# Reciprocals from a second scan that runs backwards, first-group inputs in homes of their own, and F of four units ahead of k's work

## The chip, the core and the metric

The kernel runs on one core of one Trainium2 chip. Such a core has a matrix engine (PE, with its weight loads listed apart as PEld), a vector engine (DVE), an activation engine (ACT), a general engine (POOL) and a queue engine (SP) that mostly issues DMAs; ACT can issue DMAs too. Each engine works through its own instructions in program order and waits on semaphores for the others. The metric is device time in microseconds, the median of three runs.

## The reference, cut to what matters

A recurrent attention block feeds a wide feed-forward layer. All is float32; the two weight matrices arrive as float64 words and are turned into float32 on the chip.

```
state = zeros(B, H, D, D)                      # B = 4, H = 8, D = 40
for t in range(768):
    y[t]  = r[t] @ state
    Sa    = state @ a[t]
    state = state * w[t] - outer(Sa, b[t]) + outer(v[t], k[t])
x = y as (B*S, H*D) = (3072, 320)
h = x @ w_in                                   # 320 x 2048
out = (h * clip(h + 3, 0, 6) / 6) @ w_out      # 2048 x 320
```

## The kernel before, in words

**Blocks and units.** Time is cut into blocks of 64 steps. A unit is one block of two batches, all eight heads; four units make a group, and there are 24 units in six groups. Inside a block the recurrence is rewritten with matrices: running products of w (the decays) scale a, b, k and r, the products of scaled a and b give a strictly triangular matrix F for each head, and the state's contribution needs the inverse of one plus F.

**Preparing a unit (`prepare`, lines 469 to 630).** The stages have names. W transposes w on PE, copies it into a padded tile `wm` and takes running products with a scan (line 485), `prods`. Before the change the rows of 32 steps each begin with an element that is 0 in `wm` and 1 in `start`, so one scan of 528 elements restarts in 16 rows. gam makes two tiles: `gam`, whose first half of each block is a reciprocal of products (line 496) and whose second half is a copy on POOL (497), and `rgam`, whose first half is a copy on POOL (498) and whose second half is a reciprocal (511, issued in stage A). A multiplies the transposed a by `gam` (514), B the transposed b by `rgam` (522), K the transposed k by `rgam` (606). F multiplies the results of A and B on PE (536) and copies to the tile F on ACT (542). factor turns `rgam` back and multiplies k and b with it on POOL (591). E and EV are a masked product (465) and its product with v.

**Inverting (`invert`, line 646).** Once the F of four units is there, DVE transposes it in 32 by 32 blocks (`fb`, 651), POOL masks it into `x` (654), and 60 small DVE instructions (663 and 669, in turn) invert all 32 triangles of 32 by 32 together; two more transposes give `tb` and `tt` (672, 677). `third_block` (688) then makes the missing corner of each 64 by 64 inverse on PE, ACT and POOL. The small instructions depend on one another, so others are dealt between them.

**Converting the weights (`load_weights`, line 257).** Twenty pieces of `w_in` and `w_out` are fetched as 64-bit words into spare places and converted, each by four DVE instructions (301, 321, 325, 312) and two on ACT (302, 304). A call of `next(weights)` issues one step with one of the DVE instructions. The spare places include parts of `win`, `wout`, `tinv` and of the pool `inv`. The tile of `inv` with the tag `x` is used in turn for the second set of w and a, for the matrix of the inversion and for a raw piece.

**What sets the order at the start.** Nothing is planned at run time: the order in which Python emits instructions is the order on each engine. `by_twos` (1099) walks the first group's four units through their stages, two units ahead of the other two, and appends the inversion once F of all four is emitted. From then on `aside` emits a step of the inversion at a time, and with a weight of `MIXED` a share of a conversion step. The loop at 1142 runs the inversion to its end; the numbers in `STEPS` say after which of its steps a conversion step follows. `PLAN` then lists the steps of the first group's four units (`0U` is stage U of unit 0, X and Y the two `third_block`s) and after a colon how many conversion steps follow each. From line 10 of the plan on the second group is prepared by the same `by_twos`, with feed-forward work (`pieces`) between. Later groups follow in `a_block`, in whose `together` the order of the results is the list `RESULTS`.

**Inputs.** `fetch` (383) issues two DMAs for w, a, b or k of a unit and four for r or v, on SP unless told otherwise. In the first two groups there are two sets of input tiles, for even and odd units, so the loads of units 2 and 3 are issued when units 0 and 1 have been transposed (`following`, 407). v of the first group is fetched in stage K.

Of the kernel before, what the change touches and what calls it, by code (L numbers as in the profile page):

```python
# [16 lines left out]
P = 128  # L17
BL = 64
# [12 lines left out]
def kernel(  # L31
# [145 lines left out]
    wm = const.tile([P, SCAN], F32, name="wm")  # L177
    nc.vector.memset(wm[:], 0.0)
# [40 lines left out]
    ]  # L219
    win = wts.tile([P, 2, DFF], F32, name="win")  # L220
    win2 = wts.tile([P, DFF // 2], F32, name="win2")
    wout = wts.tile([P, NJ, DM], F32, name="wout")
    WC = 256
# [159 lines left out]
    def fetch(name, i, engine=None):  # L383
# [5 lines left out]
        if name == "V":  # L389
            t = values[i % AHEAD]  # L390
        else:
            t = (others if i < 2 * NU and i % 2 and name != "R" else inputs)[name]
# [14 lines left out]
    def following(i):  # L407

        if i < 2 * NU:

            return i + 2 if i % NU < NU - 2 or i % 2 == 0 else None
        return i + 1
# [56 lines left out]
    def prepare(i, F):  # L469
        n, o = i % NU, data[i]  # L470
        halves = i >= 2 * NU
        def w_stage():
# [3 lines left out]
            wv = wm[:].rearrange("p (r m i) -> p r m i", m=2, i=HB + 1)  # L476
            x = wt[:].rearrange("p r (q m i) -> p (r q) m i", q=2, m=2)
            nc.scalar.activation(out=wv[:, :, 0, 1:HB + 1], in_=x[:, :, 0, ::-1], func=AF.Copy)
            if i == 0:
                nc.vector.tensor_copy(wv[:, :, 1, 1:HB + 1], x[:, :, 1, :])  # L480
            else:
# [4 lines left out]
                out=prods[:].rearrange("p r m i -> p (r m i)"), data0=wm[:], data1=start[:],  # L486
# [3 lines left out]
        def gam_stage():  # L490

            gam = o["G"] = grp.tile([P, NPR, P], F32, name="gam", tag="gam", bufs=NU + 2)
            rgam = o["rg"] = tmp.tile([P, NPR, P], F32, name="rgam", bufs=2)
            gv = gam[:].rearrange("p r (q i) -> p (r q) i", q=2)
            rv = rgam[:].rearrange("p r (q i) -> p (r q) i", q=2)
            nc.vector.reciprocal(gv[:, :, 0:HB], o["prods"][:, :, 0, 1:HB + 1][:, :, ::-1])  # L496
# [10 lines left out]
        def a_stage():  # L507
            x = turn_in(o["AN"], halves)
            yield PE
            rv = o["rg"][:].rearrange("p r (q i) -> p (r q) i", q=2)  # L510
            nc.vector.reciprocal(rv[:, :, HB:BL], o["prods"][:, :, 1, 1:HB + 1])  # L511
# [88 lines left out]
        def k_stage():  # L600
            x = turn_pairs(o["KN"])
            yield PE
            if i < NU:
                fetch("V", i)
            kt = o["kt"] = turned("kt")
            nc.vector.tensor_tensor(out=kt[:], in0=x[:], in1=o["rg"][:], op=ALU.mult)
# [81 lines left out]
    def third_block(F, tb, tt, n, first=False):  # L688


        zs = tmp.tile([P, 2, H, L], F32, name="zs")
# [44 lines left out]


# [361 lines left out]
    def by_twos(first, steps, mixed, rate):  # L1099
# [3 lines left out]
        for t in range(TWOS):  # L1103
# [3 lines left out]
            if t < 2:  # L1107
                order = [0, 0, 1, 1][4 * t:]
# [12 lines left out]
    for name in "WABK":  # L1121
        for i in range(2):
            fetch(name, i, (nc.sync, nc.scalar) if name == "W" else None)
    for t, _ in enumerate(by_twos(0, 4, MIXED, 0)):
        if t == 5:
            next(weights)
        limit[0] = {7: 4, 10: 12}.get(t, limit[0])
        while t == 7 and refill[0]():
            pass
        if t == RFETCH:  # L1130
            fetch("R", 0)
    ring.clear()
# [7 lines left out]
    STEPS = (1, 4, 7, 9, 12, 16, 17, 22, 27, 28, 32, 33, 34, 41, 44, 46, 51, 61, 64)  # L1140
# [15 lines left out]
    firsts = [third_block(*third[-1], n, True) for n in (0, 2)]  # L1156

    def block(i, j):

        if i % NU < 2:  # L1160
            if j == 0:
                n = i % NU
                blocks[i] = third_block(*third[-1], 2 * n)
# [4 lines left out]
    PLAN = """X X 0U:3 0UT:1 1R  # L1168
              0sn:1 0H:2 Y:1
              1U 1UT:3 0y:2  # L1170
              2RT:2 Y
              1sn 1H:1 2VT:1 0move 0move2
              1y:2 2R
              2S:1 3RT
              1move 1move2 2U:3 2UT:2 2C:4
              3R:4 3VT:3
              2rS:3 2sn:3 2H:3 3S:3
              2y:3 3U:4 3UT:2 3C:5
              3rS:3 3sn:3 3H:3 2move
              3y:1 2move2  # L1180
# [32 lines left out]
    for _ in range(18):  # L1213
# [15 lines left out]
    RESULTS = ["RT", "y", "W", "gam", "VT", "EV", "R", "S", "C", "A", "B", "move", "move2",  # L1229
               "U", "UT", "rS", "F", "K", "sn", "H", "E", "factor"]  # L1230
# [132 lines left out]
```

## Time and profile before

| what | us |
|---|---|
| median of three runs (lowest, highest) | 821.16 (818.71, 823.44) |
| the profiled execution | 820.82 |
| its span, first to last instruction | 819.1 |
| busy: PE, PEld | 742.1, 630.1 |
| busy: DVE, ACT, POOL | 534.2, 321.1, 152.4 |

The span is 1.7 us shorter than the profiled execution's time, which includes what lies around the instructions. PE is busy for 91% of the span, but not evenly: the first sixth of the span has PE mostly waiting, and after it PE is nearly full. Times inside the span are counted from its start. A group's row gives the total busy time, then the mean duration of one instruction in nanoseconds, then the idle time ahead of it with what ended that wait.

### The profile page before, as it was taken

The page shows a single profiled execution, that of the slowest core. Times are in us where ns is not written, and L with a number is a line of the kernel's source. Part 1 is how long each engine was busy: PE and PEld are TensorE (multiplying, and loading weights), DVE is VectorE, ACT ScalarE, POOL GpSimd, SP SyncE. Part 2 cuts the span into 40 slices and gives each one's busy share as a digit, 9 for nine tenths or more (in the row PEclk, how much of TensorE's full clock was granted, in tenths as well). Part 3 has the DMA queues.
Part 4 walks back from the last instruction along what each step waited for, and adds up shares of the span by engine and source line. Part 5 has one row for each costly group of instructions (what it writes and reads, how often), then busy time and mean ns, then how long its engine had stood idle before and what let it go on. Part 6 is the DMA issues. An engine that isn't in the chain of part 4 may idle for free.

```text
span 819.1 us, 35789 instructions
## 1 busy us (share of the span) xinstructions
PE 742.1 (91%) x15832; PEld 630.1 (77%) x15832; DVE 534.2 (65%) x1090; ACT 321.1 (39%) x847; POOL 152.4 (19%) x297
## 2 busy tenths in 40 slices
PE   4633858989999989999999999999999999999998
PEld 4532757868877878788888888878888888888886
DVE  8899688778855679745699564798546685232210
ACT  2233664222455423645333644334562434332211
POOL 4232101320122130322121222113112102000000
PEclk9755687999999999999999999999999999999999
DMA  6763562341223330332231233132232101100000
GB/s 111 153 150 92 122 137 59 65 67 26 42 50 62 57 62 14 60 56 48 44 57 31 46 67 56 30 57 39 41 61 53 19 20 29 29 19 16 17 19 16
DMA packets 174218, 45.05 MB, mean 55 GB/s; under 512 B 157424, under 2 KB 172784, under 8 KB 174064
## 3 DMA queue, kind: packets, MB, share of 16 engines
q1 hardware_dynamic: 171840, 42.36, 27.0%
q8 instruction: 125, 2.05, 1.1%
q10 hardware_dynamic: 2224, 0.41, 0.3%
q14 instruction: 29, 0.24, 0.1%
HBM read 34.08 MB, written 3.93 MB: 46 GB/s over the span
## 4 chain that ended last, share of the span: by engine, by line
PE 71%; issue 9%; DVE 8%; DMA 5%; SPq 3%; POOL 2%; ACT 1%; DVEq 0%; POOLq 0%; ACTq 0%
PE h L977 24%; PE o L1018 22%; PE any L456 4%; PE any L892 3%; PE any L418 3%; PE any L868 2%; PE any L428 2%; SPq L404 2%; PE any L812 1%; DVE x L669 1%; DVE prod L663 1%; PE any L773 1%; PE any L849 1%; PE any L833 1%; SPq L401 1%
## 5 line engine op out<-in xcount | busy, mean ns | idle before, releaser
L977 PE MATMUL h<-xt,win 128*128 128x128 f32 (+1 forms) x2304 | 251.6, 283 | 9.2 <-DVE gt L993 9.2
L977 PEld LDWEIGHTS h<-xt,win 128*128 128x128 f32 (+1 forms) x2304 | 232.0, 192 | 26.3 <-DVE gt L993 7.7
L1018 PE MATMUL o<-wout,gt 128*128 128x320 f32 x768 | 230.8, 444 | 0.0
L1018 PEld LDWEIGHTS o<-wout,gt 128*128 128x128 f32 x768 | 138.7, 190 | 50.5 <-issue 0.4
L992 ACT ACTIVATE gt<-h,three 128x512 f32<-128x512 f32 x96 | 62.1, 685 | 100.5 <-PE h L977 100.2
L993 DVE SCALAR_TENSOR_TENSOR gt<-gt,h 128x512 f32<-128x512 f32 x96 | 61.5, 677 | 58.4 <-ACT gt L992 57.3
L877 DVE TENSOR_TENSOR state<-any,state 40x160 f32<-40x160 f32 (+1 forms) x88 | 27.9, 321 | 67.8 <-PE any L868 41.6
L663 DVE TENSOR_TENSOR prod<-x 128x30 f32<-128x30 f32 (+9 forms) x180 | 62.3, 346 | 13.7 <-POOL x L654 8.3
L907 POOL TENSOR_TENSOR yg<-ys,gam 128x512 f32<-128x512 f32 x22 | 39.2, 1780 | 170.9 <-DVE ys L905 87.2
L669 DVE TENSOR_TENSOR x<-x,prod 128x30 f32<-128x30 f32 (+9 forms) x180 | 64.5, 359 | 5.8 <-DVE prod L663 0.5
L591 POOL TENSOR_TENSOR KBt<-K,rgt 128x320 f32<-128x320 f32 x24 | 20.9, 871 | 238.4 <-ACT rgt L581 223.6
L465 DVE COPY_PREDICATED score<-mask,any 128x256 f32<-128x256 int32 x143 | 53.3, 436 | 3.6 <-PE any L456 3.2
L496 DVE RECIPROCAL gam<-prods 128x256 f32<-128x256 f32 x24 | 41.8, 1749 | 13.6 <-POOL yg L907 13.2
L511 DVE RECIPROCAL rgam<-prods 128x256 f32<-128x256 f32 x24 | 41.8, 1743 | 0.0
L626 ACT ACTIVATE EV<-any 64x160 f32<-64x160 f32 x92 | 24.8, 296 | 40.5 <-PE any L620 31.1
L905 DVE TENSOR_TENSOR ys<-any,ys 128x256 f32<-128x256 f32 x44 | 16.6, 419 | 34.3 <-PE any L620 18.3
L485 DVE TENSOR_TENSOR_SCAN prods<-wm,start 128x528 f32<-128x528 f32 x24 | 30.0, 1248 | 10.4 <-ACT wm L482 9.9
L752 ACT ACTIVATE RT<-any 128x256 f32<-128x256 f32 (+1 forms) x44 | 15.5, 401 | 51.9 <-PE any L428 49.6
L892 PE MATMUL any<-score,KBt 64*64 64x64 f32 x1536 | 30.9, 231 | 0.2 <-DVE bt L522 0.2
L732 ACT ACTIVATE tinv<-any 32x256 f32<-32x256 f32 x48 | 17.9, 374 | 29.7 <-PE any L722 27.9
L892 PEld LDWEIGHTS any<-score,KBt 64*64 64x64 f32 x1536 | 27.2, 144 | 2.9 <-issue 0.7
L778 DVE TENSOR_TENSOR RR<-any,EV 128x160 f32<-128x160 f32 x44 | 12.2, 318 | 25.6 <-PE any L456 25.5
(181 smaller groups left out, 1058.4 us busy)
## 6 DMA issues: line engine op xcount, KB each, us to landing
B<-in_b_dram SPq DMA_DIRECT2D x48, 80.0 KB
K<-in_k_dram SPq DMA_DIRECT2D x48, 80.0 KB
V<-in_v_dram SPq DMA_DIRECT2D x96, 40.0 KB
out_dram<-ob SPq DMA_DIRECT2D x47, 80.0 KB
R<-in_r_dram SPq DMA_DIRECT2D x92, 40.0 KB
A<-in_a_dram SPq DMA_DIRECT2D x40, 80.0 KB
W<-in_w_dram SPq DMA_DIRECT2D x39, 80.0 KB
xt<-yg SPq DMA_DIRECT2D x72, 40.0 KB
```

Of the source, the lines that this page charges most:

```text
L456: nc.tensor.matmul(out=o[i][half(q), n, :], lhsT=lhs[half(i, D), n ^ (2 * q * swap), half(q)], rhs=rhs[half(i, D), n, half(q)], start=True ...
L465: nc.vector.copy_predicated(out=x[:, 4 * i:4 * i + 4, :], mask=mask4, data=o[i])
L496: nc.vector.reciprocal(gv[:, :, 0:HB], o["prods"][:, :, 0, 1:HB + 1][:, :, ::-1])
L511: nc.vector.reciprocal(rv[:, :, HB:BL], o["prods"][:, :, 1, 1:HB + 1])
L663: nc.vector.tensor_tensor(out=pv, in0=_ap(x[:], (i + 1) * L + i, [[L, n], [0, i]]), in1=_ap(x[:], i * L, [[0, n], [1, i]]), op=ALU.mult,)
L669: nc.vector.tensor_tensor(out=rest, in0=rest, in1=pv, op=ALU.add)
L892: nc.tensor.matmul(out=y[q][half(s), pr, :], lhsT=o[name][half(q), h * D:h * D + SLOT], rhs=m[name][half(q), 4 * rs + 2 * s + j, :], start ...
L907: nc.gpsimd.tensor_tensor(out=yg[:], in0=m["ys"][:].rearrange("p r q t -> p r (q t)"), in1=o["G"][:], op=ALU.mult)
L977: nc.tensor.matmul(out=hp[c][:, i, :], lhsT=lhsT, rhs=rhs, start=(begun[c] == 0), stop=(begun[c] == 3 * NQ - 1))
L992: nc.scalar.activation(out=gt[:], in_=hp[c][:], func=AF.Relu, bias=three[:], scale=1.0)
L993: nc.vector.scalar_tensor_tensor(out=gt[:], in0=gt[:], scalar=6.0, in1=hp[c][:], op0=ALU.min, op1=ALU.mult)
L1018: nc.tensor.matmul(out=op[:], lhsT=gts[c][:, n, :], rhs=wout[:, c * HJ + r * NQ + n, :], start=((split or r == 0) and c == 0 and n == 0), ...
```

## The change

Four edits go together.

1. **Reciprocals.** A second tile `wm` is added, and each has one element more. The reciprocals of 16 row ends (strided, one instruction) are written into the row heads of `start`; a scan over `wm` from its last element to its first, in place, multiplies each back by the w's; a `memset` puts the ones back. Two multiplications by 1.0 copy the results into the halves of `gam` and `rgam` that were reciprocals of 256 elements, and in stage A a `memset` of 33 elements clears the row heads of `wm`. In `RESULTS`, gam moves to the end. For unit 0 both copies of w into `wm` are made on DVE.
2. **Homes for the first group.** w, a, b and k of units 2 and 3 go into parts of `win` and `wout` that are not yet converted, their `rgam` into `win2`; four POOL memsets fill the pads. All loads of the first group are issued at the start, those of units 0 and 1 on SP and ACT alternately, and those of v after the others or between them.
3. **Order of the first group.** Lists replace `by_twos`: W, gam, A, B and F of all four units first, then the inversion begins, with K, factor, E and EV beside it.
4. **Third blocks and dealing.** The scratch `zs` of the two third blocks becomes one tile with two parts, with the tag `x`; `STEPS` has 15 numbers in place of 19, and the counts in `PLAN` are new.

```diff
+    wms = [const.tile([P, SCAN + 1], F32, name=f"wm{i}") for i in range(2)]
+    for t in wms:
+        nc.vector.memset(t[:], 0.0)
...
+    placed = {}
...
+    for i, (x, y) in enumerate([(0, DFF // 2), (0, NJ // 2)]):
+        for n, z in enumerate((x, y)):
+            t = win[:, :, z:z + H * SLOT] if i == 0 else \
+                wout[:, z:z + 4, :].rearrange("p j m -> p (j m)")[:, 0:2 * H * SLOT].rearrange(
+                    "p (n x) -> p n x", n=2)
+            t = t.rearrange("p n (h e) -> p n h e", e=SLOT)
+            name = ("WA", "BK")[i][n]
+            nc.gpsimd.memset(t[:, :, :, D:], PADS.get(name, 0.0))
+            for u in range(2):
+                placed[name, 2 + u] = t[:, u]
+    for u in range(2):
+        t = win2[:, u * NPR * P:(u + 1) * NPR * P]
+        placed["rgam", 2 + u] = t.rearrange("p (r t) -> p r t", t=P)
...
     def following(i):
 
+        if i < 2:
+            return None
...
-            nc.scalar.activation(out=wv[:, :, 0, 1:HB + 1], in_=x[:, :, 0, ::-1], func=AF.Copy)
+            if i == 0:
+                nc.vector.tensor_copy(wv[:, :, 0, 1:HB + 1], x[:, :, 0, ::-1])
+            else:
+                nc.scalar.activation(out=wv[:, :, 0, 1:HB + 1], in_=x[:, :, 0, ::-1], func=AF.Copy)
...
         def gam_stage():
 
+            prods, wm = o["prods"], o["wm"]
+            first = start[:].rearrange("p (n i) -> p n i", i=HB + 1)[:, :, 0]
+            nc.vector.reciprocal(first, prods[:].rearrange("p r m i -> p (r m) i")[:, ::-1, HB])
+            back = _ap(wm[:], SCAN, [[-1, SCAN]])
+            nc.vector.tensor_tensor_scan(out=back, data0=back, data1=start[:], initial=0.0,
+                                         op0=ALU.mult, op1=ALU.add)
+            nc.vector.memset(first, 1.0)
...
-            nc.vector.reciprocal(gv[:, :, 0:HB], o["prods"][:, :, 0, 1:HB + 1][:, :, ::-1])
+            row = 2 * (HB + 1)
+            nc.vector.tensor_scalar(gv[:, :, 0:HB], _ap(o["wm"][:], HB + 1, [[row, NB], [-1, HB]]), 1.0, None, ALU.mult)
+            nc.vector.tensor_scalar(rv[:, :, HB:BL], _ap(o["wm"][:], HB + 3, [[row, NB], [1, HB]]), 1.0, None, ALU.mult)
...
-            rv = o["rg"][:].rearrange("p r (q i) -> p (r q) i", q=2)
-            nc.vector.reciprocal(rv[:, :, HB:BL], o["prods"][:, :, 1, 1:HB + 1])
+            nc.vector.memset(_ap(o["wm"][:], 0, [[HB + 1, 2 * NB + 1]]), 0.0)
...
-            if i < NU:
-                fetch("V", i)
...
+    def third_blocks(first=False):
+
+        zs = inv.tile([P, 2, 2, H, L], F32, name="zs", tag="x", bufs=1)
+        return [third_block(*third[-1], 2 * n, zs[:, n], first) for n in range(2)]
...
-    for name in "WABK":
-        for i in range(2):
-            fetch(name, i, (nc.sync, nc.scalar) if name == "W" else None)
-    for t, _ in enumerate(by_twos(0, 4, MIXED, 0)):
-        if t == 5:
-            next(weights)
-        limit[0] = {7: 4, 10: 12}.get(t, limit[0])
-        while t == 7 and refill[0]():
+    for group, first in ("WAB", 0), ("WAB", 2), ("K", 0), ("V", 0), ("K", 2), ("V", 2):
+        for name in group:
+            for i in range(first, first + 2):
+                fetch(name, i, (nc.sync, nc.scalar) if first == 0 and name != "V" else None)
+    FIRST = "0W 1W 0gam 1gam 0A 1A 2W 3W 0B 1B 0F 1F 2gam 3gam 2A 3A 2B 3B 2F 3F".split()
+    BESIDE = "0K 1K 0factor 1factor 0E 1E 2K 3K 2factor 3factor 0EV 1EV 2E 3E 2EV 3EV".split()
+    chains = [in_turn(prepared(i), [x[1:] for x in FIRST + BESIDE if x[0] == str(i)]) for i in range(NU)]
+    for x in FIRST:
+        run(chains[int(x[0])])
+    side.append(invert(group_F[-1], third, True))
+    next(weights)
+    for n, x in enumerate(BESIDE):
+        limit[0] = {0: 4, 8: 12}.get(n, limit[0])
+        while n == 0 and refill[0]():
             pass
-        if t == RFETCH:
+        if n == 1:
             fetch("R", 0)
+        run(chains[int(x[0])], 1, MIXED if n >= 12 else 0)
...
-    STEPS = (1, 4, 7, 9, 12, 16, 17, 22, 27, 28, 32, 33, 34, 41, 44, 46, 51, 61, 64)
+    STEPS = (1, 6, 8, 9, 10, 14, 17, 25, 31, 36, 42, 48, 58, 61, 64)
...
-    firsts = [third_block(*third[-1], n, True) for n in (0, 2)]
+    firsts = third_blocks(True)
...
-    PLAN = """X X 0U:3 0UT:1 1R
-              0sn:1 0H:2 Y:1
-              1U 1UT:3 0y:2
-              2RT:2 Y
-              1sn 1H:1 2VT:1 0move 0move2
-              1y:2 2R
-              2S:1 3RT
-              1move 1move2 2U:3 2UT:2 2C:4
-              3R:4 3VT:3
-              2rS:3 2sn:3 2H:3 3S:3
-              2y:3 3U:4 3UT:2 3C:5
-              3rS:3 3sn:3 3H:3 2move
-              3y:1 2move2
+    PLAN = """X X:2 0U:3 0UT 1R
+              0sn 0H:2 Y:2
+              1U:1 1UT:3 0y:4
+              2RT:2 Y
+              1sn 1H 2VT:2 0move 0move2
+              1y:3 2R
+              2S:3 3RT
+              1move 1move2 2U:1 2UT 2C:6
+              3R:3 3VT
+              2rS:3 2sn:3 2H:4 3S:2
+              2y:2 3U:3 3UT:7 3C:5
+              3rS:4 3sn 3H 2move
+              3y 2move2
...
-    RESULTS = ["RT", "y", "W", "gam", "VT", "EV", "R", "S", "C", "A", "B", "move", "move2",
-               "U", "UT", "rS", "F", "K", "sn", "H", "E", "factor"]
+    RESULTS = ["RT", "y", "W", "VT", "EV", "R", "S", "C", "A", "B", "move", "move2",
+               "U", "UT", "rS", "F", "K", "sn", "H", "E", "factor", "gam"]
```

## The prediction, made before the changed kernel was run

> **What bounds the kernel now.** I read the slices of the page first, then the windows of ten microseconds, then DVE's timeline, last the waits. The windows (length, busy time of PE, PEld, DVE, ACT, POOL, then the granted PE clock and the DMA share) split the run in two:
>
> ```profile
> 20.00:30.00 10.00, 5.70 (x229) 4.61 (x212) 10.00 (x12) 3.38 (x12) 4.80 (x11) 1.00 0.53 80
> 30.00:40.00 10.00, 7.45 (x189) 6.21 (x193) 6.03 (x11) 1.52 (x5) 1.44 (x3) 0.55 1.05 219
> ...
> 60.00:70.00 10.00, 3.29 (x70) 2.58 (x68) 9.62 (x29) 4.19 (x7) 0.00 (x0) 0.50 0.47 97
> ...
> 90.00:100.00 10.00, 8.01 (x267) 7.19 (x266) 5.90 (x17) 5.44 (x11) 1.01 (x3) 0.66 0.70 159
> 100.00:110.00 10.00, 7.02 (x153) 6.37 (x152) 9.76 (x23) 7.65 (x14) 0.27 (x1) 0.83 0.38 91
> ...
> 190.00:200.00 10.00, 10.00 (x74) 8.49 (x73) 9.38 (x24) 1.26 (x2) 0.00 (x0) 1.00 0.04 9
> ```
>
> Until 77 us DVE is the bound: full from 10 to 30 and 40 to 80, PE mostly waiting. From 80 to 130 no engine is full: DVE is busy 36.3 of 50 us. From 140 on PE works 659.0 of 679 us; outside the last window it idles only 16.2. Of DVE time saved after 140 little can be had; the front end counts nearly in full, because the PE work behind it stays the same.
>
> DVE's timeline shows what the front consists of:
>
> ```profile
> 6.38 1.26 DVE L485 TENSOR_TENSOR_SCAN prods<-wm,start 128x528 f32<-128x528 f32 x1
> 7.67 1.75 DVE L496 RECIPROCAL gam<-prods 128x256 f32<-128x256 f32 x1
> ...
> 21.63 3.36 DVE L496 RECIPROCAL gam<-prods 128x256 f32<-128x256 f32 x2
> 24.90 1.04 DVE L465 COPY_PREDICATED score<-mask,any 128x256 f32<-128x256 int32 x3
> ...
> 33.02 0.69 DVE L606 TENSOR_TENSOR kt<-any,rgam 128x512 f32<-128x512 f32 x1 [0.55 <-PE any L418]
> 35.68 2.12 DVE L651 STREAM_TRANSPOSE fb<-F 128x1024 f32<-128x1024 f32 x1 [1.96 <-ACT F L542]
> 39.22 0.20 DVE L663 TENSOR_TENSOR prod<-x 128x30 f32<-128x30 f32 x1 [1.42 <-POOL x L654]
> ...
> 74.79 1.95 DVE L677 STREAM_TRANSPOSE tt<-x 128x1024 f32<-128x1024 f32 x1
> ```
>
> The inversion starts at 35.68 (`fb`) and ends at 76.6 (`tt` with the next start). Ahead of it stand eight reciprocals of 1.67 us start to start, and four multiplications for K and four masks that F doesn't need.
>
> [...] line 301, 512 elements, takes 0.42 us, tensor_tensor of 512 0.68. [...] the trace has 528 elements in 1.25 us. [...] while POOL multiplies for factor (41.7 to 45.5), a 108-element sum of line 669 takes 0.68 us after 0.51 idle, against 0.27 at 70.51, and line 325 takes 1.34 against 0.69. [...] the windows show 0.50 to 0.55 from 30 to 90.
>
> **Part 1, reciprocals.** Per unit two of 1.67 us go: 3.34. In their place: a reciprocal of 16 elements (256 take 1.75, a copy of 256 0.42, so some 6 ns an element and a fixed part: 0.2), a scan of 528 (1.22 start to start), a memset of 16 (0.06, line 176 has 0.07), two multiplications of 256 ([...] I take 0.27) and a memset of 33 (0.07). Sum 2.1; bounds 1.9 to 2.4. I assume that reading backwards costs nothing; no backward scan is in this trace. If it were twice as dear, 1.2 more, the gain of this part would be zero; I exclude that it speeds up. The scan[...] can now collide with POOL's three copies (0.40, 0.40, 0.21): up to 0.7 a unit, nothing at best; I take 1.0 for four units. The extra memset of `wm` (0.5) lies in DVE's idle time before 5.92.
>
> **Part 2, loads.** The w of unit 0 lands as before (PE starts at 4.38). Its two copies on DVE in turn (0.42 each, from 5.5) put the first scan at 6.4, as now. ACT issues eight DMAs at about 0.69 us from 1.1 to 6.7; unit 1's copies queue behind them and are done by 7.5, when the scan of unit 0 ends: hidden, and if late, at most 1 us. SP issues 6 + 12 + 2 + 8 + 4 + 8 = 40: 24 at 0.69 and 16 for v at 0.77 make 28.9, so the last leaves at 29.7. Now the first raw weights are issued at 29.58, so they are no later. w of units 2 and 3 leaves about 5 to 7.8 and is needed about 14; b about 10.5 to 13, needed about 22. The four pad memsets (some 1.6 us by those of 192 elements at 0.20 start to start) sit on POOL behind 6.5, ahead of unit 0's copies; these end about 9.2 and are needed for A at about 13. If PE or SP has to wait for the pads it is for something due later still.
>
> **Part 3, F first.** From 6.4: four scans 4.8, four gam parts 8.1, four memsets with A 0.63 + 0.56 x 4 ≈ 2.5, four B 2.4, collisions 1.0, in total 18.8: the last B ends at 25.2. F on PE (0.9 to 1.0) and ACT (0.66) with handovers take 1.8, so `fb` starts at 27.0 instead of 35.68: gain 8.7. The 1.42 us wait for POOL's mask is filled by two of K's multiplications.
>
> From `fb` to the end of `tt` it is 40.9 now. Two more multiplications of K (1.3) and four masks (1.4) come into it: +2.7. Of conversion steps, 19 lie there now, 9.1 us (0.48 each). After: 16 asides at the first group leave 47 numbered steps of which eleven are in `STEPS`, and the share of `MIXED` gives one: 12, so 7 fewer, -3.4. POOL's factor work doubles to eight multiplications beside the inversion; the present four cost DVE some 2.0 by the stretched rows, so +2.0. E's masks wait for PE at half clock: +0.8. Net +2.1: `tt` ends at 70.0, gain 6.6.
>
> **Part 4, plan.** The seven steps move into it: 7 x 0.53 = 3.7 us of DVE. It idles 13.7 of 50 us there, but steps in front of a mask or sum delay PE; I take half, 1.9. By the counts, the 80 steps end in the plan's line 12, not 11. A raw piece with the tag `x` now waits for the second use of `zs`; on SP, R of unit 3 stands behind it, needed three lines on: nothing, unless Y is late. Gain at the second group: 4.7.
>
> **Later units.** Twenty units save 1.2 us of DVE each, 24 us. Behind PE this is worth little: of the 16.2 us of idle, waits for DVE are part:
>
> ```profile
> PE any L620 <- issue: 4.5, 3, 3.1
> PE h L977 <- DVE gt L993: 3.6, 3, 1.3
> PE any L456 <- issue: 2.9, 3, 1.3
> ```
>
> I take 2.0; nothing to 5 is possible. Sum: 4.7 + 2.0 = 6.7 us. 820.8 (profiled execution, span 819.1 and 1.7 around it) less 6.7 is 814.1; the median stands 0.3 above the profiled one: 814.5.
>
> **Rivals.** (a) *Larger gain, 27%.* Conversion in the plan is free in DVE's idle time and later stalls close: 6.6 + 4 = 10.6, perhaps 13; about 810. For it: 13.7 us idle. Against it: ACT, which the steps load with 1.45 us a piece, is what PE waits for there (3.9 us at line 456 for U).
> (b) *No difference, 17%.* Conversion, with its DMAs, is the bound between 77 and 132 whenever the inversion ends; it now waits for raw pieces at 118 (2.9) and 123.6 (1.2). Were its end to stay at 132, the gain would be the later 2 at most: about 819.5. Against it: pieces are released by earlier conversions, which move forward too.
> (c) *Slower, 11%.* In later groups gam comes last of a stage's results, and its chain of reciprocal, scan and copies is serial; if it ends after PE's transposes of a, A and all behind it slip. The front's 6.7 is lost, and 4.1 more, when PE waits over 10.8 us in 20 units, 0.54 each; at 0.7 each the time is about 828. Against it: DVE has 35% free and the chain is 1.2 shorter than today's.
> (d) *The likeliest, 45%*: 811 to 817.
>
> The chances of (a) and (d), less a little at the edge, make 0.71 for faster by over 0.5%, about what a measurement can tell here (below 817.1); within it 0.18, slower 0.11. Range 805 to 821: below it is the far end of (a), 0.07, above it (c) and part of (b), 0.13. The bounds of scan and collisions (2 to 4 us) lie inside.
>
> **What would show it.** Backward scans of 1.25 us, multiplications of 0.2 to 0.33; `fb` at 27, `tt` ending at 70, twelve conversion steps between; the second group's first scan near 130 instead of 135.1; PE idle after 140 a little below 16. Wrong if `fb` starts after 30 because SP or ACT is late, if DVE stretches beside POOL by more than 4 us, or if the plan takes over 62 us instead of 58.5.

## The result, and the profile after

The changed kernel takes 814.54 us (median of five runs, 811.77 to 815.05). The kernel before took 821.28 in the five runs beside it. The ratio is 0.9906, with a 95% interval from 0.9876 to 0.9935: faster by 6.7 us between the medians, where 6.7 had been predicted; the interval of the ratio means 5.3 to 10.2 us, so the match to a tenth says little. Its profiled execution took 812.7 us, with a span of 811.0 (820.82 and 819.1 before). One execution of a kernel below (after, old reciprocals) was disturbed and took 2260.75 us; it is left out of that kernel's times, and its landmarks come from a second profile.

Where the time went is seen best in landmarks, in us from the span's start. The lead is how much earlier than before.

| landmark | before | after | lead | lead predicted |
|---|---|---|---|---|
| inversion starts (`fb`) | 35.68 | 26.94 | 8.7 | 8.7 |
| inversion ends (start of `tt` and its duration) | 76.7 | 71.6 | 5.1 | 6.6 |
| second group's first scan | 135.1 | 127.5 | 7.6 | 4.7 |
| second group's inversion starts | 176.2 | 171.2 | 4.9 | |
| third to sixth group's inversion starts | 287.8, 401.0, 519.5, 639.4 | 282.1, 394.2, 511.0, 631.3 | 5.7, 6.8, 8.5, 8.1 | |
| end of the span | 819.1 | 811.0 | 8.1 | 6.7 |

The windows of ten microseconds of the kernel after (length, busy time of PE, PEld, DVE, ACT, POOL, then granted PE clock, DMA share and GB/s):

```profile
20.00:30.00 10.00, 6.96 (x193) 6.29 (x182) 8.00 (x18) 2.85 (x8) 0.71 (x1) 0.88 0.49 73
30.00:40.00 10.00, 6.94 (x255) 6.38 (x250) 9.33 (x24) 3.34 (x13) 7.83 (x16) 0.97 0.64 131
60.00:70.00 10.00, 0.11 (x9) 0.14 (x13) 9.45 (x27) 1.44 (x2) 0.13 (x1) 0.50 0.07 10
90.00:100.00 10.00, 7.17 (x206) 6.16 (x206) 8.82 (x22) 6.87 (x15) 0.58 (x3) 0.83 0.70 178
100.00:110.00 10.00, 10.00 (x242) 9.61 (x241) 9.14 (x22) 7.45 (x15) 0.93 (x3) 0.83 0.36 92
```

POOL's factor work of all four units now lies beside the inversion (7.83 of 10 us from 30 to 40). From 60 to 70 PE has nothing to do. From 90 to 100 DVE is busy 8.82 where it was 5.90: the conversion steps that left the inversion fill its idle time, and DVE is now busy 43.7 of the 50 us from 80 to 130, where it was 36.3, so 6.3 of the 13.7 us of idle time are left.

DVE's timeline of the kernel after (start, duration, line, operation; in brackets the idle time ahead and what ended it):

```profile
9.88 0.26 DVE L516 RECIPROCAL start<-prods 128x16 f32<-128x16 f32 x1
10.17 1.26 DVE L518 TENSOR_TENSOR_SCAN wm<-wm,start 128x528 f32<-128x528 f32 x1
11.49 0.28 DVE L526 TENSOR_SCALAR gam<-wm 128x256 f32<-128x256 f32 x1
...
26.94 2.14 DVE L679 STREAM_TRANSPOSE fb<-F 128x1024 f32<-128x1024 f32 x1 [1.85 <-ACT F L572]
...
41.26 0.43 DVE L316 TENSOR_SCALAR parts<-tinv 128x512 uint32<-128x512 uint32 x1 [1.08 <-DMA tinv<-in_moe_w_in_dram]
58.29 0.78 DVE L483 COPY_PREDICATED score<-mask,any 128x256 f32<-128x256 int32 x2 [2.78 <-PE any L474]
69.60 2.00 DVE L705 STREAM_TRANSPOSE tt<-x 128x1024 f32<-128x1024 f32 x1
127.53 2.40 DVE L507 TENSOR_TENSOR_SCAN prods<-wm,start 128x528 f32<-128x528 f32 x2
```

The second group's first scan stood here in the kernel before:

```profile
135.11 1.26 DVE L485 TENSOR_TENSOR_SCAN prods<-wm,start 128x528 f32<-128x528 f32 x1 [1.31 <-ACT wm L482]
```

The first three lines of the kernel after are most of the new reciprocals of one unit: 0.26, 1.26 and 0.28, with a memset of 0.07 and a second multiplication of 0.29 behind them, in place of two reciprocals of 1.75. `fb` is where it was predicted. Inside the inversion stand two waits that nothing before had: 1.08 us for a raw weight, and 2.78 us for a mask whose score PE could not make. SP's timeline shows where both come from:

```profile
31.62 2.04 SPq L420 DMA_DIRECT2D W<-in_w_dram  x2
33.75 1.27 SPq L420 DMA_DIRECT2D A<-in_a_dram  x2
35.07 3.06 SPq L294 DMA_DIRECT2D tinv<-in_moe_w_in_dram  x4
38.17 1.82 SPq L294 DMA_DIRECT2D raw<-in_moe_w_in_dram  x4
40.37 3.55 SPq L417 DMA_DIRECT2D R<-in_r_dram  x4
```

The loads of w and a for the second group's first unit, released by the third unit's transposes, go out ahead of the raw weights, so these leave at 35.07 instead of 29.58, and r of unit 0, which PE needs ahead of the late mask, leaves behind them all. The four loads are 3.4 us of that delay; the 40 loads in front of them end at 31.5, 1.8 later than was forecast.

PE's waits from 126 us on in the kernel after (line, what it waited for: us in all, times, longest):

```profile
PE any L648 <- issue: 4.3, 2, 3.2
PE h L1009 <- DVE gt L1025: 4.0, 3, 1.4
PE any L924 <- DVE state L909: 3.5, 1, 3.5
```

The wait of 3.5 us for the state (line 909) falls between 126 and 140. It stands where a lead of 7.6 at the second group's first scan becomes 4.9 at its inversion: the scan comes early, but DVE then takes both units through it and through all their reciprocals before it comes to the last conversion instruction (line 327), at 135.57 where it was at 132.42 (line 312), and to the state, at 136.17. In the kernel before, half of the reciprocals of these two units came later, behind the state.

### The profile page after: what moved, and what is told of

Same layout as the page of the kernel before. It is cut to its first block, busy times and chain, and to the rows that moved or that the text cites. A ratio compares the mean times of both kernels' runs of the same rounds, so it can differ in the third digit from the quotient of the medians.

```text
span 811.0 us, 35829 instructions
## 1 busy us (share of the span) xinstructions
PE 737.0 (91%) x15832; PEld 625.2 (77%) x15832; DVE 515.8 (64%) x1188; ACT 319.8 (39%) x846; POOL 175.2 (22%) x301
## 4 chain that ended last, share of the span: by engine, by line
PE 75%; DVE 12%; DMA 4%; issue 4%; ACT 2%; SPq 2%; POOL 1%; ACTq 0%; DVEq 0%
PE h L1009 25%; PE o L1050 23%; PE any L474 4%; PE any L436 3%; PE any L924 3%; PE any L900 2%; PE any L446 2%; PE any L805 2%; DVE x L697 2%; DVE prod L691 2%; PE any L844 1%; PE any L865 1%; DVE wm L518 1%; PE any L648 1%; DMA R<-in_r_dram 1%
## 5 line engine op out<-in xcount | busy, mean ns | idle before, releaser
L909 DVE TENSOR_TENSOR state<-any,state 40x160 f32<-40x160 f32 (+1 forms) x88 | 27.9, 321 | 66.7 <-PE any L900 40.1
L621 POOL TENSOR_TENSOR KBt<-K,rgt 128x320 f32<-128x320 f32 x22 | 19.0, 866 | 222.0 <-ACT rgt L611 170.0
L654 ACT ACTIVATE EV<-any 64x160 f32<-64x160 f32 x88 | 23.9, 295 | 36.3 <-PE any L648 26.7
L518 DVE TENSOR_TENSOR_SCAN wm<-wm,start 128x528 f32<-128x528 f32 x24 | 37.6, 1567 | 0.8
L924 PE MATMUL any<-score,KBt 64*64 64x64 f32 x1536 | 31.9, 236 | 3.5 <-DVE state L909 3.5
L528 POOL COPY gam<-prods 128x256 f32<-128x256 f32 x24 | 22.5, 937 | 30.6 <-DVE prods L507 26.7
L1068 ACT ACTIVATE ob<-o 128x320 f32<-128x320 f32 x22 | 9.5, 434 | 46.3 <-PE o L1050 25.2
```

The source lines that it names most:

```text
L518: nc.vector.tensor_tensor_scan(out=back, data0=back, data1=start[:], initial=0.0, op0=ALU.mult, op1=ALU.add)
L924: nc.tensor.matmul(out=y[q][half(s), pr, :], lhsT=o[name][half(q), h * D:h * D + SLOT], rhs=m[name][half(q), 4 * rs + 2 * s + j, :], start ...
```

## The experiments

"Old" and "new" lists are `STEPS` and `PLAN` of the kernels before and after. Each ratio is to executions of the kernel before that ran beside the kernel (their medians were 820.59 to 821.96), so rows are compared better by ratios than by medians. The last column is the time that DVE waited for raw weights between 70 and 140 us, in the profiled execution; "tt ends" is the end of the inversion, "scan 2" the second group's first scan.

| kernel | median, us | ratio to before (95%) | `fb` | tt ends | scan 2 | raw waits |
|---|---|---|---|---|---|---|
| before | 821.28 | | 35.7 | 76.7 | 135.1 | 4.0 |
| after | 814.54 | 0.9906 (0.9876 to 0.9935) | 26.9 | 71.6 | 127.5 | 2.2 |
| before + new reciprocals | 822.74 | 1.0008 (0.9988 to 1.0028) | 36.5 | 77.3 | 138.2 | 6.2 |
| before + new lists | 818.56 | 0.9971 (0.9959 to 0.9983) | 35.5 | 76.0 | 133.3 | 1.0 |
| after, old reciprocals | 815.58 | 0.993 (0.9908 to 0.9951) | 31.9 | 72.1 | 128.3 | 2.8 |
| after, old ones in later groups | 813.08 | 0.9899 (0.9878 to 0.992) | 27.0 | 70.3 | 128.0 | 0 |
| after, old order of stages | 821.04 | 1.0007 (0.9994 to 1.0019) | 34.8 | 72.6 | 133.6 | 0 |
| after, old lists | 822.63 | 1.0021 (1.0009 to 1.0032) | 27.2 | 72.4 | 136.5 | 5.9 |
| the same, moves of y on POOL | 817.31 | 0.995 (0.993 to 0.997) | 26.9 | 73.6 | 132.7 | 0 |
| after, copies on ACT | 813.59 | 0.991 (0.9889 to 0.9931) | 26.9 | 69.5 | 126.0 | 0 |
| after, r earlier | 812.59 | 0.9898 (0.9875 to 0.992) | 27.3 | 70.8 | 127.0 | 2.8 |
| the same, w and a later | 812.0 | 0.9889 (0.9867 to 0.9912) | 26.9 | 68.2 | 128.0 | 5.8 |
| the same, moves of y on POOL | 809.13 | 0.9858 (0.9837 to 0.9879) | 27.0 | 67.9 | 124.9 | 0 |

One profile of a landmark isn't exact: up to the end of the inversion, DVE's work of the kernel after and of the kernel with old reciprocals in later groups alone is the same, and they end it at 71.6 and 70.3. PE's granted clock between the end of the inversion and scan 2 differs too, 0.74 and 0.68 in these two, 0.70 before, 0.67 to 0.77 in the others; no run separates it from the waits.

One landmark holds for all: in the 13 profiles of the table, each kernel's last instruction ends 682.6 to 684.8 us after its scan 2. What a kernel gains or loses, it has gained or lost by then, to about a microsecond.

**Reciprocals, each way.** First the kernel after with the old reciprocals in all 24 units and the old `RESULTS`:

```diff
-            nc.vector.reciprocal(first, prods[:]...[:, ::-1, HB])
-            back = _ap(wm[:], SCAN, [[-1, SCAN]])
-            nc.vector.tensor_tensor_scan(out=back, data0=back, data1=start[:], ...)
-            nc.vector.memset(first, 1.0)
-            nc.vector.tensor_scalar(gv[:, :, 0:HB], _ap(o["wm"][:], ...), 1.0, None, ALU.mult)
-            nc.vector.tensor_scalar(rv[:, :, HB:BL], _ap(o["wm"][:], ...), 1.0, None, ALU.mult)
+            nc.vector.reciprocal(gv[:, :, 0:HB], o["prods"][:, :, 0, 1:HB + 1][:, :, ::-1])
...
-            nc.vector.memset(_ap(o["wm"][:], 0, [[HB + 1, 2 * NB + 1]]), 0.0)
+            nc.vector.reciprocal(rv[:, :, HB:BL], o["prods"][:, :, 1, 1:HB + 1])
```

> The changed kernel with the old pairs of 256-element reciprocals in all 24 units (and gam at its old place among the results); loads, order and dealing stay new. Theory (the front end bound by DVE): each of the first four units costs 1.67 x 2 against the 2.0 measured for recip, scan, memset and two multiplications, so fb starts 4.5 to 5.5 later than 26.9, at about 31.7, and tt ends near 75; most of that reaches the end: 818 to 820. Rival A (the reciprocals are the gain, by 24 units of relief for DVE): 821 or more. Rival B (order and loads are the gain): at most 1 later, 815 to 815.5.

It took 815.58 us. The same kernel, for its landmarks:

> The changed kernel with the old pairs of reciprocals in all units again, for a profile, as the first one's was of an execution disturbed from its start. Theory: fb at 31 to 32.5 and tt ending at 75 to 76.5, 4 to 5 later than in the changed kernel, while the second group's first scan comes only 0 to 2.5 later than 127.5, because DVE's waits for raw pieces take up the rest. Rival: the delay of 4 to 5 is still there at the second group and is made good by PE later.

That one took 814.27. `fb` starts 4.9 us later, 1.2 for each of the four units, as sized. But the inversion ends 0.5 later and the second group starts 0.8 later. With `fb` at 31.9, the raw weight is there when DVE asks for it and PE has r: the waits of 1.08 and 2.78, which this kernel doesn't have, take up the lead. So these reciprocals are worth 4.9 us at `fb`, and at the end one by the medians and two by the ratios, not told apart from none.

Then the other way round, the new reciprocals in the kernel before (with its order, loads and lists; `RESULTS` and the tag of `zs` as in the change):

> The kernel before with the backward scan alone (both wm tiles and gam last among the results; the scratch zs of the third blocks moved to the tag x as in the change, to make room). Loads, order and dealing stay old. Theory: fb still cannot start before b of units 2 and 3 has landed (27.4 and 30.4 in the kernel before), so it gains at most about 1 of the 5 that DVE saves: fb at 34 to 35, the median 819 to 821. Rival A (reciprocals are the gain wherever they stand): 816 or less, fb at 31. Rival B (order and loads): 820 to 821.5.

822.74, no change that can be told. `fb` doesn't come earlier at all: what is saved in front of it turns into 2.8 us of waiting for PE's transposes of b, whose loads for units 2 and 3 leave SP at 23.9 and 26.7, behind eight of v. This line of its DVE timeline shows what the saved steps become later:

```profile
121.34 0.43 DVE L302 TENSOR_SCALAR parts<-raw 128x512 uint32<-128x512 uint32 x1 [5.99 <-DMA raw<-in_moe_w_out_dram]
```

It waits 5.99 us for the same raw piece of `w_out` that the kernel before waits 2.86 us for, here in the list of DVE's waits before (us in all, times, longest):

```profile
DVE parts L301 <- DMA raw<-in_moe_w_out_dram: 2.9, 1, 2.9
```

Third, the kernel after with the new form only in the first group (`if i < NU:` around the added lines, the old reciprocals in the other 20 units):

> The changed kernel with the backward scan in the first four units only; the 20 later units take the old reciprocals. Theory (PE bounds the run after 140, DVE's saving there is mostly hidden): 814 to 817, that is 0 to 2 slower than the changed kernel, with DVE busy 15 to 25 more in sum. Rival A (relief for DVE in all units is the gain): 818 or more. Rival C (backward scan and POOL's copies hold each other up later on, so that the new form is worse there): 812 to 814.

813.08: not slower than after, as far as can be told. DVE has 14.5 us more work (530.3 against 515.8). The profiles of all kernels show a cost of it, and what pays for it. Four have the old form in the later units (before, before + new lists, after with the old reciprocals, and this one), nine the new:

| stretch | old form | new form |
|---|---|---|
| scan 2 to the second group's inversion | 40.1 to 42.1 | 42.7 to 44.8 |
| from there to the end | 642.0 to 643.0 | 639.8 to 641.6 |
| scan 2 to the end | 682.6 to 684.3 | 683.2 to 684.8 |

So the new form saves about 2 us in the four groups that follow and gives back as much in preparing the second. There it has PE wait for the state, since both units' reciprocals stand ahead of it on DVE (3.5 us after, 2.4 in this kernel); that this is the whole reason is read from the order, not shown by a run. In sum the form of the reciprocals in the later units is no part of the gain.

**The lists.** The kernel after with the old `STEPS` and `PLAN`, all else as in the change:

> The changed kernel with the old lists for dealing conversion steps: STEPS with 19 numbers and the old counts in the plan. Theory (the step counts only shift work between the inversion and DVE's idle time in the plan): by the old STEPS 14 or 15 conversion steps lie beside the inversion instead of 12, tt ends 1 to 2 later, the plan is about that much shorter: 814 to 816. Rival (the new counts carry a good part of the gain): 818 or more.

822.63: the whole gain is gone, though `fb` starts at 27.2 and the inversion ends 4.3 us before the old one. DVE's timeline of this kernel, with the line for the same piece in the middle:

```profile
110.05 0.42 DVE L316 TENSOR_SCALAR parts<-raw 128x512 uint32<-128x512 uint32 x1
118.56 0.43 DVE L316 TENSOR_SCALAR parts<-raw 128x512 uint32<-128x512 uint32 x1 [5.90 <-DMA raw<-in_moe_w_out_dram]
121.60 1.29 DVE L1025 SCALAR_TENSOR_TENSOR gt<-gt,h 128x512 f32<-128x512 f32 x2 [2.01 <-ACT gt L1024]
```

And SP's timeline of the same kernel, ahead of that piece's load:

```profile
103.96 0.52 SPq L294 DMA_DIRECT2D raw<-in_moe_w_out_dram  x1
104.59 2.71 SPq L417 DMA_DIRECT2D R<-in_r_dram  x4
107.35 3.65 SPq L953 DMA_DIRECT2D xt<-yg  x4
111.05 3.19 SPq L958 DMA_DIRECT2D xt<-yg  x4
114.33 0.53 SPq L294 DMA_DIRECT2D raw<-in_moe_w_out_dram  x1
```

The piece can't be loaded before 114.33, because r and eight moves of y stand ahead of it on SP, at 0.7 to 0.9 us each. DVE has reached the step that converts it at 112.66, and in order it waits. Behind the waiting step stand the first feed-forward results (`gt`), for which PE waits 9.2 us. This place eats the larger part of the front's lead, as the third run of this section shows.

The new lists put into the kernel before:

> The kernel before with the new lists STEPS and PLAN alone. The changed kernel with the old lists came out at 822.6, no faster than before. Theory (the front end's lead of some 5 us and the new dealing are both needed: the lead only if DVE doesn't meet a raw piece that has not landed ahead of the first feed-forward results): the inversion ends 1 to 3 earlier than 76.6 for its fewer conversion steps, and the median is 818.5 to 821. Rival (the dealing is the gain, by itself): 816 or less. Rival (the new lists are worse without the lead): 823 or more.

818.56: 2.8 us by themselves (ratio to before 0.9971). They take 3 us of waiting for raw weights out of the plan, and the second group starts 1.9 earlier. Neither the lead nor the lists explain 6.7: with the lists, the lead is worth 4 to 5 (818.56 against 814.54, 0.9971 against 0.9906), without them, nothing.

To see whether SP's queue is what eats the lead, the kernel with the old lists was given a second queue for the 16 moves of y of units 0 and 1:

```diff
-                nc.sync.dma_start(out=dst, in_=src)
+                (nc.gpsimd if i < NP else nc.sync).dma_start(out=dst, in_=src)
```

> The changed kernel with the old lists STEPS and PLAN, and the 16 DMAs that move y of units 0 and 1 issued on POOL instead of SP. With the old lists SP issued r of unit 3 and eight of these moves from 104.6 to 114.2 without a gap, the second raw piece of w_out left at 114.3 and DVE stood 5.9 us for it, with the first feed-forward results behind. Theory (that queue on SP is what eats the front end's lead): raw pieces leave earlier, DVE's wait falls from 5.9 to under 2, the second group's first scan comes before 132 instead of 136.5, the median is 814 to 818. Rival (the raw piece waits for its place to be free, not for SP, or DVE meets something else): 820 to 823.

817.31, 5.3 us less than with the moves on SP (0.995 against 1.0021, intervals apart). The same step of DVE, in the timeline of this kernel:

```profile
114.81 0.42 DVE L316 TENSOR_SCALAR parts<-raw 128x512 uint32<-128x512 uint32 x1
```

The wait of 5.9 is gone, since the load left at 104.09 instead of 114.33. The second group starts at 132.7, 3.8 earlier, if not as early as was expected: the kernel after starts it at 127.5. With no raw weight to wait for, DVE still waits 15.1 us for PE and ACT between the end of the inversion and this scan, where the kernel after waits 9.3 for all three. So SP's queue is the larger part of what the old lists cost, and about 3 us of it have another cause that was not looked for. Issue time on SP was what was short here, and it was worth 5.3 us.

**The order of the stages.** The kernel after with the stages in the order of before: K, factor, E and EV of units 0 and 1 ahead of F of units 2 and 3:

```diff
-    FIRST = "0W 1W 0gam 1gam 0A 1A 2W 3W 0B 1B 0F 1F 2gam 3gam 2A 3A 2B 3B 2F 3F".split()
-    BESIDE = "0K 1K 0factor 1factor 0E 1E 2K 3K 2factor 3factor 0EV 1EV 2E 3E 2EV 3EV".split()
+    FIRST = "0W 0gam 1W 1gam 0A 1A 2W 0B 3W 1B 0K 1K 0factor 1factor 0F 1F 2gam 3gam 0E 1E 2A 3A 0EV 1EV 2B 3B 2K 3K 2F 3F".split()
+    BESIDE = "2factor 3factor 2E 3E 2EV 3EV".split()
```

> The changed kernel with the first group's stages in the order of the kernel before (K, factor, E and EV of units 0 and 1, and K of units 2 and 3, ahead of the last F), the new loads and reciprocals kept; beside the inversion stand factor, E and EV of units 2 and 3 with four inversion steps each, and one conversion step. Theory (DVE works as much in either order; the new order only fills its waits for F and for POOL's mask and saves nothing else): fb near 31.5, tt ends 0 to 2.5 later than 71.4, the median 814.5 to 817. Rival (F ahead of K's work is itself the gain): fb near 32 and the end 4 or more later: 818.5 or more.

821.04. `fb` starts 7.9 later than after, but the inversion ends only 1.0 later, as much as profiles differ. K and the masks cost about the same ahead of `fb` as behind it. The end is another matter: nearly all of the 6.5 us is lost in the plan, since the second group starts at 133.6, 6.0 later. Raw weights aren't the reason, as DVE waits for none there; between the end of the inversion and scan 2 it waits 15.3 us for PE and ACT, against 9.3 for all three in the kernel after. This kernel isn't clean, though. With fewer stages beside the inversion, four of its steps were dealt per stage in place of one, and conversion was one instruction behind when `tt` began (11 against 12) and two behind at 76 us (16 against 18). That the lists fit one order only is a guess; what the order alone would bring with lists of its own stays open.

**The two waits inside the inversion.** r of unit 0 is issued on ACT right after F of unit 1 (`if x == "1F": fetch("R", 0, nc.scalar)`), not behind the raw weights:

> The changed kernel with the four loads of r of unit 0 issued on ACT, in its idle time between F of units 1 and 2, instead of on SP behind the raw weights. Theory (inside the inversion DVE stands 2.8 us at the mask of unit 0's C, because r came late): that wait goes, r of unit 0 is there before 30, tt ends near 68.5 instead of 71.4, and 1.5 to 3 reach the end: 811.5 to 813. Rival (the plan's conversion sets the pace, so an earlier inversion is given back): within 0.5 of 814.5.

812.59, not told apart from after. DVE's timeline of this kernel:

```profile
43.71 0.43 DVE L316 TENSOR_SCALAR parts<-tinv 128x512 uint32<-128x512 uint32 x1 [3.13 <-DMA tinv<-in_moe_w_in_dram]
57.43 0.77 DVE L483 COPY_PREDICATED score<-mask,any 128x256 f32<-128x256 int32 x2
```

The mask no longer waits, so r was its cause. But the wait for the first raw piece is 3.13 instead of 1.08: one wait took the other's place. SP's timeline of this kernel shows that, with r on ACT's queue, SP's own issues fell behind:

```profile
19.62 5.86 SPq L417 DMA_DIRECT2D V<-in_v_dram  x5
38.35 2.02 SPq L294 DMA_DIRECT2D tinv<-in_moe_w_in_dram  x4
```

The first eight issues of v took 8.84 us (6.01 in the kernel after), and the raw weights left at 38.35 instead of 35.07. So in a second kernel w and a of unit 4 were also kept out of the way (`if i != 2:` before the two `fetch` calls in W and A, and both units loaded in the plan):

> As the run with r of unit 0 loaded early on ACT, and w and a of unit 4 loaded later, in the plan with those of unit 5, so that their four issues no longer stand on SP ahead of the raw weights. In the run with r alone the wait of 2.8 us for r went and a wait of 3.1 for the first raw piece came in its place. Theory (SP's queue sets when the first raw piece lands): raw issues start near 31.6 instead of 35.1, the piece lands near 40, the wait of DVE for it falls below 0.5, tt ends near 68, and the median is 810 to 812. Rival (a third wait takes the place, or the plan gives it back): 812 to 814.5, no difference from the run with r alone.

812.0. The raw weights leave at 34.35, 4.0 earlier than with r alone, if not near 31.6 as was expected, and 0.7 of the wait for them is left. Now the inversion ends at 68.2, 3.4 earlier than after, and still the second group starts no earlier (128.0). In the plan DVE waits again:

```profile
114.23 0.43 DVE L316 TENSOR_SCALAR parts<-raw 128x512 uint32<-128x512 uint32 x1 [2.88 <-DMA raw<-in_moe_w_out_dram]
120.48 0.43 DVE L316 TENSOR_SCALAR parts<-raw_fb 128x512 uint32<-128x512 uint32 x1 [2.41 <-DMA raw_fb<-in_moe_w_out_dram]
```

It is the same mechanism as with the old lists, in smaller size. So the two cures belong together: this kernel with the moves of units 0 and 1 on POOL.

> The changed kernel with r of unit 0 early on ACT, w and a of unit 4 late, and the moves of y of units 0 and 1 on POOL. With the first two alone the inversion ended 3.4 us earlier than in the changed kernel, at 68.2, but the median was 812.0. Theory (the lead is given back at the raw pieces behind SP's queue): with the moves off SP, 2 to 4 more are kept: 808 to 810.5. Rival (the plan's conversion is bound by DVE itself): 811 to 813.

809.13 (808.69 to 811.64), 0.9858 of before, 5.4 us below after by the medians and 3.9 by the ratios. No raw weight is waited for in the plan, and the second group starts at 124.9, where it was 127.5. It is faster than both kernels in the medians; against the kernel after, the intervals (up to 0.9879, from 0.9876) just touch. The kernel after with the moves on POOL alone was not run, so what each of the three edits brings here isn't told apart.

**Copies of gam.** The backward scan took 1.26 us in the first group but 1.57 on the mean of all 24, and POOL's copy to `gam` (line 528) 0.94 where it had been 0.40. Are the copies what the scan collides with? They were put on ACT:

```diff
-            nc.gpsimd.tensor_copy(gv[:, :, HB:BL], o["prods"][:, :, 1, 0:HB])
-            nc.gpsimd.tensor_copy(rv[:, :, 0:HB], o["prods"][:, :, 0, 0:HB][:, :, ::-1])
+            nc.scalar.activation(out=gv[:, :, HB:BL], in_=o["prods"][:, :, 1, 0:HB], func=AF.Copy)
+            nc.scalar.activation(out=rv[:, :, 0:HB], in_=o["prods"][:, :, 0, 0:HB][:, :, ::-1], func=AF.Copy)
```

> The changed kernel with the two copies of 256 elements into gam and rgam on ACT instead of POOL, in all units. Theory (scan and copies hold each other up, but behind PE): the backward scans fall from a mean of 1.57 to 1.3, DVE's sum by some 7 and POOL's by some 40, and the median stays within 1.5 of 814.5. Rival A (this collision eats the gain of the later units): 811 to 813. Rival B (ACT, on which PE waits, pays for it): 816 or more.

813.59, the same, and the scans are as long as ever (37.4 us in all). The copies were the ones held up, not the cause. The timeline of the kernel after has another candidate, POOL's multiplication for `yg`:

```profile
353.56 1.25 DVE L507 TENSOR_TENSOR_SCAN prods<-wm,start 128x528 f32<-128x528 f32 x1
353.72 2.15 POOL L939 TENSOR_TENSOR yg<-ys,gam 128x512 f32<-128x512 f32 x1 [4.92 <-DVE ys L937]
355.13 1.85 DVE L518 TENSOR_TENSOR_SCAN wm<-wm,start 128x528 f32<-128x528 f32 x1
355.93 1.25 POOL L528 COPY gam<-prods 128x256 f32<-128x256 f32 x1
```

From 289 us on, each of the 12 backward scans takes 1.85 to 1.87 us, and at each one a `yg` runs that had started 1.4 to 1.5 us before it. In the 12 before that none does, and they take 1.26 to 1.33. `yg` takes 2.15 there and 1.27 alone. In each of these overlaps the instruction that starts second is the one that takes longer: `yg` behind the forward scan (0.9 us), the backward scan behind `yg` (0.6 us), the copy behind the backward scan (0.85 us); the forward scan, which starts first, keeps its 1.25. So the first seems to hold up the second. It is read from coincidence, not from a run without `yg`; with the copies on ACT the means stayed as they were, 1.56 for the scan and 1.77 for `yg`.

## Why the prediction was right or wrong

**Part 1, the reciprocals.** The sizes were right: a unit's five instructions in gam take 2.02 us from start to start (9.88 to 11.90), and the memset in stage A, which has 17 elements and not 33, takes 0.07 beside other work, against 2.1 in all. The backward scan took 1.26 us, as did the forward one of unit 0. The 0.27 for a multiplication of 256 elements was the author's estimate; half of what 512 took before (0.42 on line 301, 0.68 for a tensor_tensor) would put it between 0.21 and 0.34, and in the first group it took 0.27 to 0.29. That the new reciprocals bring `fb` 4.9 us forward is shown by the kernel with the old ones; that this reaches the end is not. Two terms were wrong and made each other good, which is luck in the forecast of `fb` (26.94 against 27.0). The collision of the scans with POOL's copies was sized at 1.0 for four units, an estimate too, but the four backward scans took 1.26 to 1.27 and one forward scan 1.42. And unit 1's copies on ACT, taken as hidden or "at most 1 us", had DVE wait 0.82.

**Part 2, the loads.** Wrong in one sentence: "Now the first raw weights are issued at 29.58, so they are no later." The 40 issues were counted, and took 1.8 us more than the 28.9 forecast; the four of w and a for unit 4, which the third unit's transposes release, were not, and took 3.4. The raw weights left 5.5 later, and r behind them. The two waits, 1.08 and 2.78, are the bill. With 0.7 left of both, the inversion ended at 68.2 and the time was 812.0, so the price at the end was below what can be told.

**Part 3, F first.** `fb` was right. The stretch from there to the end of the inversion was forecast at 43.0 and took 44.7 (43.4 in the kernel that differs only in later groups). Two unforeseen waits of 3.9 in all were in it, so what was sized (four masks and two multiplications, POOL, PE at half clock (0.50 from 40 to 80 us before), seven steps fewer) came to some 2 less than its terms. Twelve conversion steps lie there, as forecast. The two terms that came to nothing are POOL's and PE's. The 60 small instructions did take 22.3 us beside POOL's doubled work, where they took 20.7, but two conversion instructions that were longer beside POOL's work before (1.34 in place of 0.69 beside factor, 1.47 in place of 0.42 beside a memset) have no counterpart, so the 2.0 put on POOL is about zero. And no mask of E waited for PE, on which 0.8 had been put.

**Part 4, the plan.** Here the reasoning failed, although the total came out. The new counts were taken as a cost of 1.9 on the lead ("The seven steps move into it: 7 x 0.53 = 3.7 us of DVE [...] I take half, 1.9"). The lead at the second group was not 4.7 but 7.6. The stretch from the end of the inversion to that scan, 58.4 before, didn't grow by 1.9 but shrank to 55.9 (57.6 in the kernel that differs only in later groups). DVE works 2.9 more in it and waits 9.3 in place of 14.7, for raw weights, PE and ACT together (10.8 in the other kernel, none of it for raw weights). So the steps that moved stand in time that DVE would have waited out. The runs show that the lists are the condition of the gain: with the old ones the same front end gives 822.63.

**Later units.** Predicted 2.0. The stretch that was meant is there in the profiles: from the second group's inversion on, the new form is about 2 us shorter, but it gives that back between scan 2 and this inversion, so in sum it brought none, and the kernel that keeps the old reciprocals took 813.08. Some of the loss in size is `yg`, which takes back 0.6 of 1.2 us in 12 units. Of the three waits of PE shown for this term only one is a wait for DVE (3.6 us for `gt`), and it didn't fall (4.0). The sum came to 6.7 because 2.9 more at the second group stood against 2.0 that came and went; that is luck. It also explains the leads of the first table, 7.6, then 4.9, then 8.1 at the end; the medians differ by 6.7, so part of the 8.1 is the one execution.

**The rivals.** (a), that conversion in the plan is free, had the better mechanism: its steps did fall into idle time. Its 810 was not reached; DVE still waited 2.2 us for raw weights there, and the kernel without these waits, whose inversion also ends 3.7 earlier, took 809.13. (b), no difference because conversion's DMAs bind, was real: it is most of what happens with the old lists, at 822.6. "Against it: pieces are released by earlier conversions, which move forward too" was wrong as to the reason, because a piece that is released also needs its turn on SP: with the old lists one left at 114.33, with the moves of y off SP at 104.09. (c), gam last in later groups, left no trace: the ten profiles with gam last take 639.8 to 642.0 us from the second group's inversion to the end, the three with gam in its old place, all with the old reciprocals, 642.6 to 643.0.

## What to carry to other kernels

An early front end is worth only what the waits behind it leave of it, here above all those for a DMA: after moving a stage, follow the load that the following stage asks for to its place in the issuing queue, and count everything ahead of it, issues released by other stages included. The place of a step that may wait in its engine's order decides who waits with it (behind the 5.9 us that DVE stood, PE stood 9.2); here a list of counts was worth as much as eight microseconds, and 16 issues on another queue five. Another queue is no free place either: with four loads on ACT's, eight issues of SP's took 2.8 us more. Two edits that each do little or nothing alone (2.8 and none) can need each other, so undo them one at a time from both ends. And look for the landmark behind which all versions take the same time; here it was the second group's first scan.

## What was not expected of the hardware

A backward scan in place took as long as a forward one (1.26 us for 528 elements, both in the first group). In a chain of three overlaps of DVE and POOL, scan, `yg`, scan, copy, each behind the first took longer than alone (`yg` 2.15 in place of 1.27, the scan 1.85 in place of 1.26, the copy 1.25 in place of 0.40); taking the copy out of it moved no time that could be told, and the rest was not tried. The issue of one DMA mostly occupied SP for 0.4 to 0.9 us, the moves of y 0.61 to 0.91, and in the plan that was scarce rather than the transfers: the DMA share from 100 to 110 was 0.36. Issues on one queue went together with slower ones on another: with r of unit 0 on ACT, eight issues of v on SP took 8.84 us (8.75 with w and a of unit 4 later) instead of 6.01.
